# One store of the normalized tokens instead of four, and value and query weights loaded by rows of 128

## The chip, the cores and the metric

The kernel runs on one core of one Trainium2 chip. The metric is device time in microseconds (us) for one execution. Undisturbed executions of one kernel agree within one to one and a half per cent. Some are slow: they take over 1.5% more time than the fastest.

A ratio in this text is the mean time of one kernel's fast runs over the mean time of the other's fast runs of the same rounds on the same chip. It is not quite the ratio of the medians that are also quoted. The bracket behind a ratio is its 95% interval.

The engines are called by their short names in the profile. PE is TensorE, PEld its weight load, DVE VectorE, ACT ScalarE, POOL GpSimd, and SP SyncE, which computes nothing here and issues transfers. A "q" behind a name (SPq) means the engine's instruction queue.

## The reference

The input is 2,048 tokens of width 640 in bf16. One layer norm feeds two branches, and both are added to the input.

```python
def reference(x, wqkv, wo, w_gate, w_up, w_down):
    xn = layernorm(x)                        # 2048 x 640
    # A: 32 heads of 20; each token looks at itself and 7 earlier
    #    tokens, 2 apart; softmax over these 8
    q, k, v = split(xn @ wqkv)
    logits[h, s, w] = scale * sum_d q[h, s, d] * k[h, s - 2 * w, d]
    o = sum_w softmax(logits)[h, s, w] * v[h, s - 2 * w]
    # B: gated, without a nonlinearity; width 1536
    h = (xn @ w_gate) * (xn @ w_up)
    return x + o @ wo + h @ w_down
```

## The kernel before

The tokens go through in 4 chunks of 4 tiles; a tile is 128 tokens. At build time a small list scheduler in Python fixes each engine's order of instructions by estimated times. On the chip each engine then runs its list strictly in order: an instruction that waits holds up everything behind it on its engine.

The parts that matter here are these. First, the opening loads, all on SP's queue. `N2` is 320, so the value weights come as two halves of the columns of 400 KB each.

```python
    load_x(0, (0, 1))     # token tiles, 160 KB each
    load_v(0)             # value weights, first half of the columns
    load_x(0, (2,))
    load_v(N2)
    load_x(0, (3,))
    load_qkv(0)           # query weights, one transfer of 800 KB
    load_qkv(1)           # key weights
    load_x(1)
```

Second, the normalized tokens. In chunk 0 TensorE transposes them (`pst`). In chunks 1 to 3 each tile is stored to DRAM (`xnD`), and one DMA transpose reads the whole chunk back (`xnT`).

```python
def scale_x():
    xn_t = cpool.tile([P, D], BF, name="xn_t")      # 2 buffers
    nc.vector.tensor_scalar(xn_t[:], x_tiles[c * CH + ttl][:], ...)
...
def keep():                                         # once for each tile
    nc.sync.dma_start(out=xnD[tg * P : (tg + 1) * P, :], in_=st["xn", ttl][:])
    if ttl == CH - 1:
        later.append((turn_all, lambda t=clock["dve"]: t + 3.0))

def turn_all():
    nc.sync.dma_start_transpose(out=st["xnT"][:], in_=xnD[chunk c] ...)
    done["turned", c] = min(clock["pe"], clock["dve"])
```

Third, what follows the transpose of chunk 1 on the queues: the tokens of chunk 2 on SP's queue, and on POOL's software queue the output weights and down weights, 2.7 MB in all, which are called the late weights here.

```python
later.append((lambda: (load_x(2), load_down()), when(("turned", 1))))
```

`turned` is a time in the scheduler's estimate. On the chip SP waits for the store before it issues the transpose.

The attention weights. VectorE forms the products of queries and shifted keys (`pw`, six buffers), TensorE sums them by head (`lps`), ScalarE takes the exponential (`e`), VectorE masks the edge, and TensorE spreads `e` back to tokens (`eT`). On VectorE's list, the statistics and scalings of chunk 2 stand before the mask of chunk 0. A scaling that waits therefore delays the first spread.

The softmax here doesn't subtract the row's maximum and nothing guards it: scores larger than these inputs give would overflow.

Of the kernel before, what the change touches and what calls it, by code (L numbers as in the profile page):

```python
# [9 lines left out]
BF = dt.bfloat16  # L10
# [7 lines left out]
def kernel(  # L18
# [11 lines left out]
    nc = tc.nc  # L30
    P = nc.NUM_PARTITIONS
# [3 lines left out]
    S, D = x_flat.shape  # L35
# [9 lines left out]
    KT = D // P  # L45
    FT = F // P
    NT = S // P
    CH = 4
    NCH = NT // CH
    CS = CH * P  # L50
    JL = P // H
    N2 = D // 2
# [35 lines left out]
    xnD = dram.tile([S, D], BF, name="xnD")  # L88
# [4 lines left out]
    def load_x(c, ttls=range(CH)):  # L93
        for ttl in ttls:
            tg = c * CH + ttl
            x_t = cpool.tile([P, D], BF, name="x_t", bufs=6)
            nc.sync.dma_start(out=x_t[:], in_=x_flat[tg * P : (tg + 1) * P, :])
            x_tiles[tg] = x_t
# [2 lines left out]
    wg_r = B_w_gate.rearrange("(i p) f -> p i f", p=P)  # L101
    wu_r = B_w_up.rearrange("(i p) f -> p i f", p=P)

    def load_qkv(r):
        nc.sync.dma_start(
            out=wqkv[:, :, r * D : (r + 1) * D], in_=wqkv_r[:, :, r * D : (r + 1) * D]
        )

    def load_v(n0):
        cols = slice(2 * D + n0, 2 * D + n0 + N2)  # L110
        nc.sync.dma_start(out=wqkv[:, :, cols], in_=wqkv_r[:, :, cols])

    load_x(0, (0, 1))
    load_v(0)
    load_x(0, (2,))
    load_v(N2)
    load_x(0, (3,))
    load_qkv(0)
    load_qkv(1)
    load_x(1)  # L120

# [64 lines left out]
    main, chain = deque(), deque()  # L186
    burst, quick, later = [], [], []
    done = {}
    rings = {"mm": (4, []), "tr": (2, []), "lg": (1, []), "e": (1, [])}

    def when(*names):
        return lambda: max((done.get(n, INF) for n in names), default=0.0)
# [45 lines left out]
    def norm(c, group):  # L238
        st = state[c]
        st["xnT"] = None  # L240

        def alloc():
            if st["xnT"] is None:
                st["xnT"] = cpool.tile([P, KT, CS], BF, name="xnT", bufs=3)

        def steps(t0):
            g = {}

            def stats():
                g["mv"] = cpool.tile([P, group, nc.vector.BN_AGGR_DIM], F32, name="mv", bufs=2)  # L250
                for k in range(group):
                    x_t = x_tiles[c * CH + t0 + k]
                    s = cpool.tile([P, 2, nc.vector.BN_STATS_DIM], F32, name="stats")
                    for hf in range(2):
                        nc.vector.bn_stats(s[:, hf, :], x_t[:, hf * N2 : (hf + 1) * N2])  # L255
                    nc.vector.bn_aggr(g["mv"][:, k, :], s[:])
                rstd = cpool.tile([P, group], F32, name="rstd", bufs=2)
                nc.gpsimd.tensor_scalar(rstd[:], g["mv"][:, :, 1], EPS, None, op0=ALU.add)
                nc.gpsimd.tensor_tensor(
                    rstd[:], rstd[:], mhalf[:].to_broadcast([P, group]), ALU.pow  # L260
                )
                g["rstd"] = rstd

            def stats_after(t):
                on("pool", ("rstd", c, t0), t + LAG, 0.85)

            op(chain, ("stats", c, t0), stats, 1.12 * group, None, stats_after)

            def scaling(ttl, k):
                def scale_x():  # L270
                    xn_t = cpool.tile([P, D], BF, name="xn_t")
                    nc.vector.tensor_scalar(  # L272
                        xn_t[:], x_tiles[c * CH + ttl][:],
                        scalar1=g["mv"][:, k, 0:1], scalar2=g["rstd"][:, k : k + 1],
                        op0=ALU.subtract, op1=ALU.mult,
                    )
                    st["xn", ttl] = xn_t

                def turn():
                    alloc()  # L280
                    pst = ps_tr.tile([P, KT, P], BF, name="pst", tag="tr")
                    for i in range(KT):
                        nc.tensor.transpose(
                            pst[:, i, :], st["xn", ttl][:, i * P : (i + 1) * P], ident
                        )
                    nc.scalar.copy(st["xnT"][:, :, tcols(ttl)], pst[:])
                    if c == ttl == 0:
                        warm_up(14)

                def turned(t):  # L290
                    on("act", ("xnT", c, ttl), t + LAG, 0.7)

                def keep():
                    tg = c * CH + ttl
                    nc.sync.dma_start(
                        out=xnD[tg * P : (tg + 1) * P, :], in_=st["xn", ttl][:]
                    )
                    if ttl == CH - 1:
                        later.append((turn_all, lambda t=clock["dve"]: t + 3.0))

                def turn_all():
                    alloc()
                    nc.sync.dma_start_transpose(
                        out=st["xnT"][:],
                        in_=xnD[c * CS : (c + 1) * CS, :].rearrange("m (k p) -> m k p", p=P),
                    )
                    done["turned", c] = min(clock["pe"], clock["dve"])
                    for k in range(CH):
                        done["xnT", c, k] = done["turned", c] + 8.0

                def scaled(t):
                    if c >= 1:
                        later.append((keep, lambda t=t: t))
                        return
                    op(burst, ("turn", c, ttl), turn, 0.3, when(("xn", c, ttl)), turned,
                       ("tr", ("xnT", c, ttl)), 0.7)

                def later_free():
                    old = done.get(("turn", c, ttl - 2), INF)
                    if c >= 1:  # L320
                        old = done.get(("xn", c, ttl - 2), INF) + 3.0
                    return max(done.get(("rstd", c, t0), INF), old if ttl >= 2 else 0.0)

                op(chain, ("xn", c, ttl), scale_x, 0.43, later_free, scaled)

            return [lambda k=k: scaling(t0 + k, k) for k in range(group)]

        if group == 1:
            prev = None
            for t0 in range(CH):  # L330
                cur = steps(t0)
                if prev:
                    prev[0]()
                prev = cur
            prev[0]()
        else:
            for t0 in range(0, CH, group):
                for f in steps(t0):
                    f()
# [85 lines left out]
    def weights(c):  # L425
        st = state[c]
        for g in range(2):
            for j in range(JL):

                def product(g=g, j=j):  # L430
                    off = DIL * (JL * g + j)
                    pt = apool.tile([P, KT, CS], BF, name="pw", tag="pw", bufs=6)
                    nc.vector.tensor_tensor(  # L433
                        pt[:], st["qT"][:], st["kT"][:, :, off : off + CS], ALU.mult
                    )
                    st["pw", g, j] = pt

                def heads(g=g):
                    if g == 0:
                        st["e"] = apool.tile([P, 2, CS], BF, name="e", bufs=1)  # L440
                    lps = ps_log.tile([P, CS], F32, name="lps", tag="lg")
                    for i in range(KT):
                        for j in range(JL):
                            nc.tensor.matmul(  # L444
                                lps[H * j : H * (j + 1), :], lhsT=Ek[:, i, :],
                                rhs=st["pw", g, j][:, i, :],
                                start=(i == 0), stop=(i == KT - 1),
                                tile_position=(0, H * j), skip_group_check=True,
                            )
                    nc.scalar.activation(st["e"][:, g, :], lps[:], ACT.Exp, scale=scale)  # L450

                def headed(t, g=g):
                    on("act", ("exp", c, g), t + LAG, 0.6)

                def after(t, g=g, j=j, heads=heads, headed=headed):
                    if j == JL - 1:
                        op(burst, ("heads", c, g), heads, 1.2, when(("pw", c, g, j)), headed,
                           ("lg", ("exp", c, g)), 0.7)

                n = (c * 2 + g) * JL + j - 6  # L460
                free = ("heads", n // (2 * JL), n // JL % 2) if n >= 0 else None
                need = [("qk", c, 1, KT - 1)] + ([free] if free else [])
                op(chain, ("pw", c, g, j), product, 1.43, when(*need), after)

    def attend(c, ttls):
        st = state[c]
# [258 lines left out]
```

## Time and profile before

| | before |
|---|---|
| median of the first 6 runs | 272.94 us (272.09 to 274.74) |
| profiled span | 271.7 us |
| PE busy | 262.8 us, 97% |
| first query matmul on PE | 14.59 us |
| PE waits for products (`lps`) | 1.08 and 0.46 us |
| PE waits for the first spread (`eT`) | 1.76 us |
| DVE waits for stores of tokens | 14.7 us |

The first part of the profile of the kernel before gives busy time, share of the span and number of instructions for each engine.

```profile
PE 262.8 (97%) x1656; PEld 146.3 (54%) x1656; DVE 198.1 (73%) x278; ACT 101.7 (37%) x181; POOL 35.2 (13%) x77
```

PE is nearly full, so only its gaps can be won. The view of waits, for PE in the kernel before, lists them. Its columns are the waiting line, what it waited for, then the total in us, how often, and the longest.

```profile
PE eT L477 <- DVE e L469: 1.8, 1, 1.8
PE lps L444 <- DVE pw L433: 1.5, 2, 1.1
...
PE pst L283 <- DVE xn_t L272: 0.9, 1, 0.9
PE pst L283 <- POOL rstd L258: 0.4, 1, 0.4
```

The first two lines are waits for VectorE in the middle of the kernel; the last two belong to the start-up. The groups view of the kernel before tells why VectorE is late. Behind the first bar stand busy us and mean ns, behind the second the idle us before the group and what ended most of it.

```profile
L272 DVE TENSOR_SCALAR xn_t<-x_t,mv,rstd 128x640 bf16<-128x640 bf16 x16 | 6.9, 439 | 18.6 <-DMA xnD<-xn_t 14.7
```

With two buffers, the third scaling waits until the first store has landed. The timeline of DVE before, in chunk 1, shows this one by one. Columns are start, duration, instruction, and in brackets the idle time before it with its releaser.

```profile
18.76 0.80 DVE L272 TENSOR_SCALAR xn_t<-x_t,mv,rstd 128x640 bf16<-128x640 bf16 x2 [1.44 <-POOL rstd L259]
25.51 0.45 DVE L272 TENSOR_SCALAR xn_t<-x_t,mv,rstd 128x640 bf16<-128x640 bf16 x1 [5.95 <-DMA xnD<-xn_t]
28.81 0.45 DVE L272 TENSOR_SCALAR xn_t<-x_t,mv,rstd 128x640 bf16<-128x640 bf16 x1 [2.86 <-DMA xnD<-xn_t]
29.17 2.89 DVE L433 TENSOR_TENSOR pw<-qT,kT 128x2560 bf16<-128x2560 bf16 x2
```

Four scalings of 0.4 us are spread over more than 10 us, and the products of chunk 0 stand behind them. The timeline of SP's queue before shows the other end. A duration here is how long an issue holds the queue.

```profile
19.23 10.39 SPq L295 DMA_DIRECT2D xnD<-xn_t  x4
36.48 2.74 SPq L303 DMA_TRANSPOSE xnT<-xnD  x1
39.27 2.20 SPq L97 DMA_DIRECT2D x_t<-in_A_x_dram  x4
```

Stores, transpose and the load of chunk 2 follow each other in order. The transpose could not be issued before the last store had landed.

### The profile page before, as it was taken

What the parts mean: (1) busy time and instruction counts of PE and PEld (TensorE: products, weight loads), DVE (VectorE), ACT (ScalarE), POOL (GpSimd) and SP (SyncE); (2) the same over time, 40 slices, a digit from 0 to 9 for tenths busy, and PEclk for the clock granted to TensorE, in tenths of its full rate; (3) what the DMA queues carried; (4) which work ended last, traced back from release to release, by engine and by line L of the source; (5) the groups of instructions that cost most, each with busy time, mean ns of one, the idle gap of its engine ahead of it and who ended that gap; (6) DMA issues with size and microseconds to landing.
All of it is one profiled execution on the core that took longest, in us unless ns stands there. A gap on an engine that the chain in (4) does not pass through costs nothing.

```text
span 271.7 us, 4250 instructions
## 1 busy us (share of the span) xinstructions
PE 262.8 (97%) x1656; PEld 146.3 (54%) x1656; DVE 198.1 (73%) x278; ACT 101.7 (37%) x181; POOL 35.2 (13%) x77
## 2 busy tenths in 40 slices
PE   7899989979999999999999999999999999999995
PEld 7544434434645667544443577744446774445773
DVE  4460798299999965996999399799949999622221
ACT  2655545535655300255454510045551004555000
POOL 3748000200000041200000003020000212000100
PEclk9999999999999999999999999999999999999999
DMA  7999979746999925599877029959500796110111
GB/s 212 364 395 368 308 153 334 261 117 193 250 320 214 276 54 201 122 286 246 171 203 138 24 94 270 282 172 274 143 2 0 231 274 198 48 27 0 48 51 48
DMA packets 50069, 50.11 MB, mean 184 GB/s; under 512 B 20499, under 2 KB 47713, under 8 KB 50049
## 3 DMA queue, kind: packets, MB, share of 16 engines
q1 hardware_dynamic: 44704, 35.72, 49.1%
q0 software_dynamic: 3040, 11.49, 13.0%
q10 hardware_dynamic: 2304, 2.62, 2.9%
q8 instruction: 13, 0.21, 0.3%
q14 instruction: 8, 0.06, 0.1%
HBM read 35.39 MB, written 9.85 MB: 166 GB/s over the span
## 4 chain that ended last, share of the span: by engine, by line
PE 46%; DVE 26%; DMA 20%; issue 4%; SPq 2%; POOL 1%; DVEq 0%; POOLq 0%
PE psf L624 14%; PE psu L575 10%; PE psg L575 10%; DMA xnD<-xn_t 9%; PE psf L617 6%; DVE pw L433 6%; DMA x_t<-in_A_x_dram 4%; DMA v_1435<-vD 4%; DVE stats L255 3%; DMA v_912<-vD 3%; PE psv L388 2%; PE lps L444 2%; PE psqk L362 2%; DMA out_dram<-osb 1%; DVE xn_t L272 1%
## 5 line engine op out<-in xcount | busy, mean ns | idle before, releaser
L575 PE MATMUL psu<-xnT,wu 128*128 128x512 bf16 x240 | 59.7, 379 | 0.0
L575 PE MATMUL psg<-xnT,wg 128*128 128x512 bf16 x240 | 59.6, 379 | 0.0
L624 PE MATMUL psf<-wd,hT 128*128 128x320 bf16 x384 | 57.6, 299 | 0.0
L580 ACT CAST gs<-psg 128x512 bf16<-128x512 f32 x48 | 28.1, 585 | 76.1 <-PE psg L575 74.3
L433 DVE TENSOR_TENSOR pw<-qT,kT 128x2560 bf16<-128x2560 bf16 x32 | 46.1, 1485 | 0.0
L624 PEld LDWEIGHTS <-hT 128*128 128x128 bf16 x384 | 37.5, 98 | 14.9 <-issue 0.4
L362 PE MATMUL psqk<-xnT,wqkv 128*128 128x512 bf16 x200 | 44.3, 379 | 0.0
L575 PEld LDWEIGHTS <-wu 128*128 128x128 bf16 x240 | 23.2, 98 | 28.4 <-issue 1.3
L580 ACT CAST us<-psu 128x512 bf16<-128x512 f32 x48 | 28.1, 585 | 27.6 <-PE psu L575 27.6
L575 PEld LDWEIGHTS <-wg 128*128 128x128 bf16 x240 | 23.3, 98 | 27.5 <-issue 0.4
L362 PEld LDWEIGHTS <-wqkv 128*128 128x128 bf16 x200 | 19.4, 98 | 23.0 <-issue 0.4
L585 DVE TENSOR_TENSOR hT<-gs,us 128x512 bf16<-128x512 bf16 x48 | 19.7, 419 | 16.5 <-ACT us L580 16.3
L631 DVE TENSOR_TENSOR osb<-psf,xr 128x320 bf16<-128x320 f32 x32 | 15.2, 485 | 19.6 <-PE psf L624 14.2
L617 PE MATMUL psf<-wo_perm,oT 128*128 128x320 bf16 x160 | 27.0, 299 | 0.0
L641 POOL DMA_DIRECT2D out_dram<-osb x13 | 7.1, 545 | 142.3 <-DVE osb L631 139.5
L388 PE MATMUL psv<-wqkv,xnT 128*128 128x320 bf16 x160 | 23.6, 299 | 0.0
L272 DVE TENSOR_SCALAR xn_t<-x_t,mv,rstd 128x640 bf16<-128x640 bf16 x16 | 6.9, 439 | 18.6 <-DMA xnD<-xn_t 14.7
L388 PEld LDWEIGHTS <-xnT 128*128 128x128 bf16 x160 | 15.2, 98 | 6.9 <-issue 0.8
L617 PEld LDWEIGHTS <-oT 128*128 128x128 bf16 x160 | 15.5, 98 | 5.9
L255 DVE BATCH_NORM_STATS2 stats<-x_t 128x6 f32<-128x320 bf16 x32 | 13.6, 468 | 6.1 <-DMA x_t<-in_A_x_dram 6.1
L394 ACT CAST v_t<-psv 128x320 bf16<-128x320 f32 x32 | 13.6, 425 | 8.0 <-PE psv L388 6.1
L368 ACT CAST qT<-psqk 128x512 bf16<-128x512 f32 x20 | 11.7, 585 | 10.2 <-PE psqk L362 10.2
(106 smaller groups left out, 194.2 us busy)
## 6 DMA issues: line engine op xcount, KB each, us to landing
x_t<-in_A_x_dram SPq DMA_DIRECT2D x16, 160.0 KB, 3.4
vD<-v_t ACTq DMA_DIRECT2D x16, 160.0 KB, 5.3
xr<-in_A_x_dram POOLq DMA_DIRECT2D x16, 160.0 KB, 3.5
out_dram<-osb POOLq DMA_DIRECT2D x13, 160.0 KB, 3.0
wg<-in_B_w_gate_dram POOLq DMA_DIRECT2D x2, 960.0 KB, 9.8
wu<-in_B_w_up_dram POOLq DMA_DIRECT2D x2, 960.0 KB, 12.9
xnD<-xn_t SPq DMA_DIRECT2D x12, 160.0 KB, 4.4
wd<-in_B_w_down_dram POOLq DMA_DIRECT2D x1, 1920.0 KB, 11.4
```

The costliest lines, as they stand in the source:

```text
L255: nc.vector.bn_stats(s[:, hf, :], x_t[:, hf * N2 : (hf + 1) * N2])
L362: nc.tensor.matmul(ps[:], lhsT=wqkv[:, i, r * D + j * P : r * D + (j + 1) * P], rhs=st["xnT"][:, i, :], start=(i == 0), stop=(i == KT - 1),)
L368: nc.scalar.copy(dst[:, j, o : o + CS], ps[:])
L388: nc.tensor.matmul(ps[:, 0:N2], lhsT=st["xnT"][:, i, tcols(ttl)], rhs=wqkv[:, i, 2 * D + n0 : 2 * D + n0 + N2], start=(i == 0), stop=(i == ...
L394: nc.scalar.copy(v_t[:].rearrange("p (j h) -> p j h", j=Dh)[:, :, k * HH : (k + 1) * HH], ps[:, 0:N2].rearrange("p (h j) -> p j h", j=Dh),)
L433: nc.vector.tensor_tensor(pt[:], st["qT"][:], st["kT"][:, :, off : off + CS], ALU.mult)
L575: nc.tensor.matmul(ps[:], lhsT=w[:, i, f * P : (f + 1) * P], rhs=st["xnT"][:, i, :], start=(i == 0), stop=(i == KT - 1),)
L580: nc.scalar.copy(s[:], ps[:])
L585: nc.vector.tensor_tensor(h[:], st["gu", 0, f][:], st["gu", 1, f][:], ALU.mult)
L617: nc.tensor.matmul(ps[:, 0:N2], lhsT=st["oT", ttl][:, i, :], rhs=wo_perm[:, i, n0 : n0 + N2], start=(i == 0), stop=False,)
L624: nc.tensor.matmul(ps[:, 0:N2], lhsT=st["hT", f][:, tcols(ttl)], rhs=wd[:, f, n0 : n0 + N2], start=False, stop=(f == FT - 1),)
L631: nc.vector.tensor_tensor(osb[:, n0 : n0 + N2], ps[:, 0:N2], xr[:, n0 : n0 + N2], ALU.add)
```

## The change

The change has two halves that do not depend on each other. The compute is the same.

- **Store half.** In chunks 1 to 3 the four scalings write into one buffer of four tiles, which takes a place in the ring of the product buffers. One store of 640 KB replaces four of 160 KB. VectorE should no longer wait for stores.
- **Load half.** Value weights and query weights come in five transfers of 160 KB each, one for each block of 128 rows, so that TensorE can begin with the first block. Token tiles 2 and 3 now stand behind all value weights.

```diff
-    def load_qkv(r):
-        nc.sync.dma_start(
-            out=wqkv[:, :, r * D : (r + 1) * D], in_=wqkv_r[:, :, r * D : (r + 1) * D]
-        )
-    def load_v(n0): ...
+    def load_qkv(r, rows=False):
+        cols = slice(r * D, (r + 1) * D)
+        for i in range(KT) if rows else (slice(0, KT),):
+            nc.sync.dma_start(out=wqkv[:, i, cols], in_=wqkv_r[:, i, cols])
 
     load_x(0, (0, 1))
-    load_v(0)
-    load_x(0, (2,))
-    load_v(N2)
-    load_x(0, (3,))
-    load_qkv(0)
+    load_qkv(2, True)
+    load_x(0, (2, 3))
+    load_qkv(0, True)
     load_qkv(1)
     load_x(1)
 ... (in scale_x)
-                    xn_t = cpool.tile([P, D], BF, name="xn_t")
+                    if c < 1:
+                        xn_t = cpool.tile([P, D], BF, name="xn_t")
+                    else:
+                        if ttl == 0:
+                            st["xn"] = apool.tile([P, CH, D], BF, name="xn", tag="pw", bufs=6)
+                        xn_t = st["xn"][:, ttl, :]
 ... (in keep, now called once for each chunk)
-                        out=xnD[tg * P : (tg + 1) * P, :], in_=st["xn", ttl][:]
+                        out=xnD[c * CS : (c + 1) * CS, :].rearrange("(t p) d -> p t d", p=P),
+                        in_=st["xn"][:],
                     )
-                    if ttl == CH - 1:
-                        later.append((turn_all, lambda t=clock["dve"]: t + 3.0))
+                    later.append((turn_all, lambda t=clock["dve"]: t + 4.0))
 ... (the scheduler's ring for "pw" buffers, and its uses, left out)
```

Since the scheduler's estimates change, the orders on PE, DVE and ACT change a little too: on PE, head sums and spreads stand earlier.

## The prediction

> **What bounds the kernel.** TensorE. The page gives PE 262.8 of 271.7 us (97%) at full granted clock, and the windows view has it 100% busy in nearly every 20 us stretch from 60 to 240 us. So only PE's gaps are for sale. The timeline of PE lists them: start-up (first real matmul at 6.95 us, the eight value groups not done before 14.6 us, with idles of 0.44, 0.93 us), 1.08 us before the first head-sum matmuls at 35.6 us (waits for VectorE's product), 1.76 us before the first spread at 56.2 us (waits for the mask), 0.46 us at 145.3 us, and the tail after 268.7 us, which the change leaves alone. Sum of what could be won: about 4.5 us, 1.7%.
>
> **Why the gaps exist.** The first two mid-kernel gaps come from VectorE, in order behind a normalized-token write whose two buffers wait for stores. The groups view charges 14.7 us of VectorE idle to these stores; the timeline shows 5.95 and 2.86 us in chunk 1 (18.8 to 29.3 us), 4.70 in chunk 2, 1.15 in chunk 3.
>
> **What changes.** Chunks 1 to 3 write four tokens into one buffer and one 640 KB store replaces four of 160 KB; VectorE writes all four in about 1.8 us. Compute is equal. Instruction order: value/query weights take 10 queue issues instead of 3 (0.43 to 0.53 us each); spreads and head sums stand earlier on PE, by 2 to 8 us.
>
> 1. Products of chunk 0 no longer start at 29.2 us but when the keys are copied (about 26 us): three us earlier. The 1.08 us gap should vanish.
> 2. The store of chunk 1 still crawls. From 18 to 37 us the DMA view shows the software queue moving 5.20 MB in 1,288 packets (4.0 KB each), SP's queue 0.66 MB in 576 (1.1 KB each). The Trainium skill ("DMA: Bandwidth & Descriptors", Queues, rings and completion order) says that an engine alternates between queues by whole packets; the trace agrees in direction, since 160 KB took 6.3 and 7.0 us here against 1.8 us at best. One store took 6.3, two 9.2 us; extended, my estimate for 640 KB is 8 to 15 us: landing at 29 to 36 us, before 36.3. So the transpose, the load of chunk 2 and its statistics come 0 to 6 us earlier, and VectorE, ready at about 39 us, may wait for that load. The spread stands at about 48 us on PE and the mask comes at 47 to 49 us: of 1.76 us I expect 0.9 to 1.76 back.
> 3. Start-up: rows of 1,280 bytes should move faster than half rows of 640 (295 to 324 GB/s before, 367 later), but token tile 2 now queues behind all value weights (about 1 us later), and VectorE scales tile 1 only after it; tile 3 arrives about 0.6 us sooner. I count 0, plus or minus 0.6 us.
> 4. VectorE then runs 6 to 9 us ahead, but the schedule also moves PE's consumers up, so the 0.46 us gap at 145 us may stay or grow to about 1 us; value gathers (6 to 10 us each) are unchanged.
>
> Sum: 1.1 + 1.4 + 0 + 0.1 = about 2.6 us. **Predicted 270.3 us, range 268.0 to 272.8.** Faster by over 2%: 0.03; within: 0.94; slower: 0.03.
>
> **Signs.** Right: no VectorE wait on these stores; no PE wait for products near 34 us; the wait before the first spread under 1 us; PE busy time unchanged; first query matmul at 14 to 15.2 us. Wrong: a new PE wait at transposes of tile 1 near 8 us, or at head sums of chunks 1 to 3.
>
> **What would break it.** The single store landing after 37 us; value weights arriving after 8 us; head sums scheduled earlier than value gathers allow; clock throttling.

## The result, and the profile after

| | before | after |
|---|---|---|
| median of all runs beside each other | 273.55 us (40 runs, 271.51 to 275.28) | 272.64 us (20 runs, 271.09 to 293.04) |
| ratio of fast runs | | 0.9961 [0.9937, 0.9986] |
| slow runs | 0 of 40 | 3 of 20 |
| profiled span | 271.7 us | 269.4 us |
| first query matmul | 14.59 us | 15.65 us |
| last matmul group starts | 266.84 us | 264.40 us |

By the threshold of 2% the two kernels are the same. The gain is 0.4%, 1.1 us, where 2.6 us had been forecast. The profile shows 2.3 us, but the profiled execution of the changed kernel was a quick one: it took 271.46 us by the clock, against a median of 272.64, while that of the kernel before took 273.79 us against 273.55. The profile's sums are therefore used for where time went, and the timed ratios for how much.

The first part of the profile after.

```profile
PE 262.7 (98%) x1656; PEld 146.8 (54%) x1656; DVE 198.0 (73%) x278; ACT 101.8 (38%) x181; POOL 35.3 (13%) x77
```

The work is the same to 0.1 us. The waits of PE after:

```profile
PE pst L282 <- DVE xn_t L271: 1.7, 2, 1.4
...
PE eT L474 <- DVE e L466: 0.6, 1, 0.6
```

The wait for products is gone, that for the spread is down to 0.6 us, and a larger wait stands at the start-up transposes. The timeline of DVE after, to be held beside the four lines of before:

```profile
20.78 1.52 DVE L271 TENSOR_SCALAR xn<-x_t,mv,rstd 128x640 bf16<-128x640 bf16 x4 [1.44 <-POOL rstd L253]
27.26 2.90 DVE L432 TENSOR_TENSOR pw<-qT,kT 128x2560 bf16<-128x2560 bf16 x2 [4.96 <-ACT kT L367]
```

Four scalings run in 1.52 us, and VectorE then waits for the keys, not for a store. The head sums show an effect that the list of waits understates. The timeline of PE before has both of its waits inside a group of 20 head-sum matmuls:

```profile
34.11 0.40 PE L444 MATMUL lps<-pw,Ek 128*32 128x512 bf16 x3
35.59 1.24 PE L444 MATMUL lps<-pw,Ek 128*32 128x512 bf16 x17 [1.08 <-DVE pw L433]
...
144.46 0.40 PE L444 MATMUL lps<-pw,Ek 128*32 128x512 bf16 x3
145.31 1.24 PE L444 MATMUL lps<-pw,Ek 128*32 128x512 bf16 x17 [0.46 <-DVE pw L433]
```

The same group after, on the same engine:

```profile
35.17 1.26 PE L443 MATMUL lps<-pw,Ek 128*32 128x512 bf16 x20
```

In one piece the group takes 1.26 us. Broken in two it lasted from 34.11 to 36.83 and from 144.46 to 146.55 us, 2.72 and 2.09 us. So the two breaks cost 1.46 and 0.83 us, not 1.08 and 0.46. With this the profile adds up: 2.3 us at the head sums and 1.1 us at the spread (1.76 to 0.64), less 1.1 us at the start (14.59 to 15.65), make 2.3 us. The last matmul group starts 2.4 us earlier.

The start-up is where time was lost. Two timelines of the kernel before, first PE and then DVE, up to 16 us:

```profile
7.64 0.44 PE L283 MATMUL pst<-selb,xn_t 128*128 128x128 bf16 x5
9.70 0.45 PE L283 MATMUL pst<-selb,xn_t 128*128 128x128 bf16 x5 [0.93 <-DVE xn_t L272]
14.59 10.96 PE L362 MATMUL psqk<-xnT,wqkv 128*128 128x512 bf16 x50
```

```profile
6.05 0.89 DVE L255 BATCH_NORM_STATS2 stats<-x_t 128x6 f32<-128x320 bf16 x2 [0.39 <-DMA x_t<-in_A_x_dram]
13.16 0.89 DVE L255 BATCH_NORM_STATS2 stats<-x_t 128x6 f32<-128x320 bf16 x2 [2.31 <-DMA x_t<-in_A_x_dram]
```

And the same two of the kernel after:

```profile
9.39 0.45 PE L282 MATMUL pst<-selb,xn_t 128*128 128x128 bf16 x5 [1.44 <-DVE xn_t L271]
10.76 0.45 PE L282 MATMUL pst<-selb,xn_t 128*128 128x128 bf16 x5 [0.24 <-DVE xn_t L271]
15.65 10.96 PE L361 MATMUL psqk<-xnT,wqkv 128*128 128x512 bf16 x50
```

```profile
7.89 0.89 DVE L249 BATCH_NORM_STATS2 stats<-x_t 128x6 f32<-128x320 bf16 x2 [2.23 <-DMA x_t<-in_A_x_dram]
15.19 0.89 DVE L249 BATCH_NORM_STATS2 stats<-x_t 128x6 f32<-128x320 bf16 x2 [3.28 <-DMA x_t<-in_A_x_dram]
```

The statistics of token tile 2 begin at 7.89 instead of 6.05 us, since the tile now queues behind all value weights. VectorE scales tile 1 only after them, so the transpose of tile 1 on PE moves from 7.64 to 9.39 us, and the first query matmul is 1.06 us later. The first value matmul, which was meant to begin earlier with the first block of weights, came at 7.10 us against 6.95 before. The second DVE line is the arrival of chunk 1's tokens, 2.0 us later. The windows view tells of the rate. Its columns are the window, its length, busy us (with instructions) of PE, PEld, DVE, ACT and POOL, then granted clock, DMA share and GB/s. Before:

```profile
6.00:8.00 2.00, 2.00 (x29) 1.63 (x26) 1.41 (x4) 0.85 (x2) 1.01 (x3) 1.00 1.03 324
8.00:10.00 2.00, 1.07 (x13) 0.62 (x11) 1.42 (x4) 1.23 (x3) 0.74 (x3) 1.00 1.06 368
```

After:

```profile
6.00:8.00 2.00, 1.95 (x25) 1.33 (x22) 0.11 (x1) 0.70 (x2) 0.36 (x1) 1.00 0.90 271
8.00:10.00 2.00, 0.61 (x8) 0.54 (x9) 1.97 (x6) 0.54 (x2) 0.81 (x2) 1.00 0.96 282
```

The rows move at 271 to 282 GB/s, the large transfers moved at 324 to 368. From 3 to 6 us it is 260 against 295. These are single profiles: over all profiles of this case, the stretch from 8 to 10 us has 282 to 348 GB/s with rows and 361 to 379 without. Last, SP's queue after:

```profile
22.33 0.40 SPq L293 DMA_DIRECT2D xnD<-xn  x1
30.25 8.88 SPq L301 DMA_TRANSPOSE xnT<-xnD  x1
39.19 2.58 SPq L97 DMA_DIRECT2D x_t<-in_A_x_dram  x4
```

The store landed early: the transpose is issued at 30.25 us, 6.2 us sooner than before. But it now holds the queue for 8.88 us instead of 2.74, up to the moment at which the down weights land (39.1 us), and the load behind it starts at 39.19, where it had started at 39.27. All that the early store had won for the next chunk was lost again in one instruction.

### The profile page after: what moved, and what is told of

Read it like the earlier page. It is cut to its first block, busy times and chain, and to the rows that moved or that the text cites. A ratio compares the mean times of both kernels' runs of the same rounds, so it can differ in the third digit from the quotient of the medians.

```text
span 269.4 us, 4231 instructions
## 1 busy us (share of the span) xinstructions
PE 262.7 (98%) x1656; PEld 146.8 (54%) x1656; DVE 198.0 (73%) x278; ACT 101.8 (38%) x181; POOL 35.3 (13%) x77
## 4 chain that ended last, share of the span: by engine, by line
PE 80%; DMA 9%; SPq 4%; DVE 4%; POOL 1%; issue 1%; POOLq 0%
PE psf L621 19%; PE psu L572 15%; PE psg L572 15%; PE psqk L361 12%; PE psf L614 8%; PE psv L387 6%; DMA x_t<-in_A_x_dram 6%; SPq L301 3%; DMA xnD<-xn 3%; PE lps L443 3%; DVE stats L249 2%; DVE xn L271 1%; SPq L107 1%; POOL rstd L253 1%; DVE mv L250 1%
## 5 line engine op out<-in xcount | busy, mean ns | idle before, releaser
L621 PEld LDWEIGHTS <-hT 128*128 128x128 bf16 x384 | 37.5, 98 | 14.4
L387 PEld LDWEIGHTS <-xnT 128*128 128x128 bf16 x160 | 15.3, 98 | 6.6 <-issue 0.4
L367 ACT CAST kT<-psqk 128x512 bf16<-128x512 f32 x20 | 11.7, 585 | 10.2 <-PE psqk L361 10.2
```

Of the source, the lines that this page charges most:

```text
L367: nc.scalar.copy(dst[:, j, o : o + CS], ps[:])
L387: nc.tensor.matmul(ps[:, 0:N2], lhsT=st["xnT"][:, i, tcols(ttl)], rhs=wqkv[:, i, 2 * D + n0 : 2 * D + n0 + N2], start=(i == 0), stop=(i == ...
L621: nc.tensor.matmul(ps[:, 0:N2], lhsT=st["hT", f][:, tcols(ttl)], rhs=wd[:, f, n0 : n0 + N2], start=False, stop=(f == FT - 1),)
```

## The experiments

Three things were open. First, which half brings the gain and which takes it away. Second, within the load half, whether the new order or the split into rows is to blame. Third, why the transpose of chunk 1 became slow: because one big store precedes it, or because it now runs side by side with the late weights, which were nearly through by the time the old transpose was issued (POOL issued them from 23.8 to 27.2 us before and from 26.0 to 29.4 us after, and the largest took 11 us to land). Each variant kept the order of instructions on PE, DVE and ACT of the kernel that it was made from, except for the moved issues of transfers.

### Both halves apart

**The changed kernel once more**, beside the variants, on their chip.

> The changed kernel once more, on the chip of its siblings, to see how much of the profiled 2.3 us (271.7 to 269.4 us of span) is a lucky profile. My theory: the change won 1.08 (head sums), 1.1 (spread) and 0.46 us and lost 1.06 us at start-up, so a true gain of 1.0 to 2.3 us; ratio 0.992 to 0.997, span of the profile 269 to 271 us. Rival: the profiled execution was an outlier and some gaps come back in other executions: then this profile has a product or spread wait over 1 us again.

It measured 272.23 us, ratio 0.9952 [0.9918, 0.9987]; its profile spans 269.3 us, with the first query matmul at 15.75 us, the spread wait at 0.4 us and a transpose of 10.2 us. One of six runs was slow (294.71 us). The result repeats.

**The kernel before with the new loads only.**

```diff
 # kernel before, plus the load half
-    load_v(0); load_x(0, (2,)); load_v(N2); load_x(0, (3,)); load_qkv(0)
+    load_qkv(2, True); load_x(0, (2, 3)); load_qkv(0, True)
```

> The kernel before with only the new load order. Theory: the loads alone cost about 1 us: first query matmul near 15.6 us against 14.6 us, wait at the transposes of tile 1 near 1.4 us, ratio 1.002 to 1.005. Rival: loads are neutral and start-up scatters by a microsecond anyway: first query matmul 14.4 to 15 us, ratio 0.999 to 1.001.

It measured 274.67 us, ratio 1.0051 [1.0006, 1.0096]: the load half alone makes the kernel before slower by 1.4 us. The waits of PE:

```profile
PE eT L471 <- DVE e L463: 2.6, 1, 2.6
PE pst L277 <- DVE xn_t L266: 1.8, 2, 1.6
PE lps L438 <- DVE pw L427: 1.4, 1, 1.4
```

The waits for the spread and at the start-up transposes are longer than before; that for products is 1.4 us once, where it was 1.08 and 0.46 us. Its profile fell on the slowest of its six runs (277.04 us), so the 2.6 may be at the upper end; a repeated profile of the kernel before had 2.6 there as well.

**The changed kernel with the old loads**, that is the store half alone.

```diff
 # changed kernel, loads as before
-    load_qkv(2, True); load_x(0, (2, 3)); load_qkv(0, True)
+    load_v(0); load_x(0, (2,)); load_v(N2); load_x(0, (3,)); load_qkv(0)
```

> The changed kernel with the old load order (column halves of the value weights, token tiles 2 and 3 in between). Theory: gains add up: first query matmul back at 14.6 us, no product wait, spread wait under 1.2 us; ratio to before 0.988 to 0.993, about 1 us better than the changed kernel. Rival: an earlier start only moves the waits: the spread waits 1 us longer, and the time stays that of the changed kernel, 0.995 to 0.997.

It measured 270.62 us, ratio 0.9909 [0.9872, 0.9946]. That is 2.5 us of 273.25 (the median of before in these rounds), nearly the whole forecast of 2.6. Its waits of PE:

```profile
PE pst L288 <- DVE xn_t L277: 1.3, 2, 0.8
...
PE eT L480 <- DVE e L472: 0.2, 1, 0.2
```

No wait for products, 0.2 us at the spread, and the first query matmul at 14.43 us. So the store half, with the order that goes with it, does what was hoped, and the load half takes back 1.2 us (0.9952 against 0.9909) to 1.4 us.

### Order or split

**The new order, but value and query weights in one transfer each.**

```diff
-    load_qkv(2, True)
+    load_qkv(2)
     load_x(0, (2, 3))
-    load_qkv(0, True)
+    load_qkv(0)
```

> The changed kernel with value and query weights by one transfer each instead of five, in the same order (tiles 2 and 3 behind the whole value weights). It parts the split from the order. If the split costs (many issues, lower rate; windows showed 260 to 282 GB/s at 3 to 10 us against 295 to 368 before): tile 2 lands at 6.8 to 7.2 us instead of 7.9, first query matmul near 14.6 to 15 us, chunk 1 tokens land before 14 us instead of 15.2. If the order costs: tile 2 still at 7.6 us or later and the first query matmul at 15.3 us or later.

It measured 271.29 us, ratio 0.9935 [0.9899, 0.9972]. The timeline of DVE has the two arrivals:

```profile
7.81 0.89 DVE L249 BATCH_NORM_STATS2 stats<-x_t 128x6 f32<-128x320 bf16 x2 [2.13 <-DMA x_t<-in_A_x_dram]
...
13.49 0.89 DVE L249 BATCH_NORM_STATS2 stats<-x_t 128x6 f32<-128x320 bf16 x2 [1.66 <-DMA x_t<-in_A_x_dram]
```

Token tile 2 is as late as with rows (7.81), and the first query matmul too (15.57). But chunk 1's tokens arrive at 13.49, 1.7 us sooner than with rows, the stream runs at 314 to 368 GB/s between 6 and 10 us, and the spread does not wait. So there are two costs: the order delays the start, and the split into rows slows the stream, which chunk 1 feels. Whether the split costs through smaller transfers or through the issues (SP needs about 0.46 us for each of ten, instead of for two) was not tested.

**Rows, but with the token tiles between them**, the fourth corner.

```diff
         for i in range(KT) if rows else (slice(0, KT),):
+            if r == 2 and i in (2, 4):
+                load_x(0, (1 + i // 2,))
             nc.sync.dma_start(out=wqkv[:, i, cols], in_=wqkv_r[:, i, cols])
-    load_x(0, (2, 3))
```

> The changed kernel, value and query weights still by rows of 128, but token tile 2 after the second of the five value rows and tile 3 after the fourth, about as they stood before the change. It completes the square of split and order. Theory (two costs: the order delays tile 2 and so the value groups; the split slows the stream and so chunk 1's tokens): statistics of tile 2 start near 6.1 to 6.8 us instead of 7.9, first query matmul at 14.6 to 15.2 us instead of 15.4 to 15.9, while chunk 1's tokens still land at 14.8 us or later; ratio to before 0.991 to 0.994. Rival (the split alone costs, order does not): tile 2 still at 7.4 us or later and the first query matmul at 15.4 us or later; ratio 0.995 or more.

It went wrong in a way that nothing here had foretold: five of six runs were slow, the median was 280.68 us (271.08 to 286.26), and no ratio could be formed. The early part can still be read: tile 2 at 6.27 us and the first query matmul at 14.62, as with the old order, and chunk 1's tokens at 15.33, as with rows. The fast profile of these loads with later weights, below, agrees: 5.72, 14.41 and 15.43 us. The two costs are separable. The slowness had to be looked at by itself, below.

By time the order costs about 0.7 us (0.9909 to 0.9935) and the split about 0.5 us (0.9935 to 0.9952). The intervals of these ratios overlap, so neither of the two is clear of noise by itself. Two versions with rows and with the late weights issued later, both described below, part the order once more, on different chips: 0.9923 with the tiles between, 0.9985 with them behind. What makes the partition more than a guess is the times in the traces. In the six profiles whose tile 2 queues behind all value weights its statistics begin at 7.6 to 8.1 us and the first query matmul comes at 15.4 to 15.9 us; in the ten others these are 5.7 to 6.8 and 14.4 to 15.3. In the eight profiles with rows chunk 1's tokens arrive at 15.2 to 16.2 us, in the eight others at 13.0 to 13.9.

**Both tiles between the two halves of the value weights**, on the store half alone.

```diff
 # store half alone
     load_v(0)
-    load_x(0, (2,))
+    load_x(0, (2, 3))
     load_v(N2)
-    load_x(0, (3,))
```

> Old loads with the collected store, but tokens 2 and 3 both before the second half of the value weights. Theory (start-up is set by when tile 3 has landed, since VectorE takes its statistics before it scales tile 2): tile 3 lands near 7.3 us instead of 8.0, first query matmul about 0.3 to 0.4 us earlier (14.0 to 14.2 us), ratio 0.001 lower than that of the collected store with old loads. Rival: the second half of the value weights becomes the limit near 8 us: a wait at the second value group, first query matmul at 14.4 us or later.

It measured 270.17 us, 0.9895 [0.9863, 0.9927]; the first query matmul stayed at 14.53 us and the spread waited 1.1 us in this profile. This is not to be told from the store half alone.

### Why the transpose was slow

**The late weights issued later**, after the statistics of chunk 2 in VectorE's list.

```diff
-    later.append((lambda: (load_x(2), load_down()), when(("turned", 1))))
+    later.append((lambda: load_x(2), when(("turned", 1))))
 ...
     norm(2, 4)
+    side(load_down)
```

> The changed kernel with the output and down weights (2.7 MB, on the software queue) issued after the statistics of chunk 2 instead of beside the store and transpose of chunk 1. Theory: that traffic made the transpose of chunk 1 hold SP's queue for 8.9 to 10.2 us; without it the issue takes 2.6 to 3.0 us as in the other chunks, the load of chunk 2 starts at 31 to 34 us instead of 39 to 40.5, VectorE no longer waits for it (3.1 to 3.4 us before), the mask is written by about 48 us and the spread wait (0.4 to 0.6 us) is gone; time 0.4 to 0.6 us better than the changed kernel, ratio to before about 0.993. Rival: the transpose is slow because it follows a single big store; then it still takes 8 us or more.

SP's queue in this variant:

```profile
30.81 2.65 SPq L301 DMA_TRANSPOSE xnT<-xnD  x1
33.52 1.99 SPq L97 DMA_DIRECT2D x_t<-in_A_x_dram  x4
...
54.31 6.96 SPq L301 DMA_TRANSPOSE xnT<-xnD  x1
```

Without late weights beside it the transpose of chunk 1 takes 2.65 us, and the load of chunk 2 is out at 33.52 instead of 39.19. The store before it is the same single one of 640 KB, so the store is not the cause. POOL issued the late weights at 46.2 to 49.7 us instead, and the slow transpose moved to chunk 2 (6.96 us). The traces show one thing more. In all ten fast profiles in which a transpose is issued over 3 us before the down weights land, it holds the queue until the down weights land, within 1.3 us (39.13 and 39.1 us in the changed kernel, 61.27 and 60.6 us here). How long it holds the queue thus followed how much of the weights was left. The new wait is on PE, at the head sums of chunk 1:

```profile
86.79 1.24 PE L443 MATMUL lps<-pw,Ek 128*32 128x512 bf16 x17 [1.03 <-DVE pw L432]
```

VectorE was late there because it had waited 3.2 us for a gather of values (the shifted values of a tile, read back from DRAM) until 68.9 us; it was issued on SP's queue after the slow transpose. The spread did not wait any more, but the time was 272.63 us, ratio 0.9985 [0.9945, 1.0026]: nothing won. The weights have to pass somewhere, and at both places tried they met a transpose and SP's queue stood.

**The same on the store half alone.**

> Old load order, collected store, and late output and down weights: all three findings together. Theory: start-up as before the change (first query matmul 14.4 to 14.6 us), no product wait, no spread wait; but the collected store with old loads had only 0.2 us of spread wait left, so the time is at most 0.3 us better than that kernel: ratio to before 0.988 to 0.991. Rival: weights that move beside the value gathers of chunk 0 (42 to 56 us) delay these, and a new wait appears on VectorE before the first mixes or on TensorE at the head sums of chunk 1: ratio 0.992 or more.

It measured 272.37 us, 0.9967 [0.9934, 0.9999], worse than 0.9909 without the edit. The transposes of chunks 1 and 2 took 2.69 and 7.27 us, and PE waited 1.4 us for products near 85 us. The pattern is the same.

**The tokens of chunk 2 issued ahead of the transpose**, on the changed kernel.

```diff
 # in keep, after the store
+                    if c == 1:
+                        load_x(2)
 ...
-    later.append((lambda: (load_x(2), load_down()), when(("turned", 1))))
+    later.append((load_down, when(("turned", 1))))
```

> The changed kernel with the load of chunk 2's tokens issued before the transpose of chunk 1 rather than behind it; all other traffic as it was. Theory: VectorE's wait of 3.1 to 3.4 us for those tokens vanishes, whatever the transpose does (its issue stays 8 us or more, or grows, since the tokens move beside it); the spread wait vanishes; ratio about 0.993. Rival: what holds the spread is something else (the value weights' late start), then the spread wait stays at 0.4 us or more although the tokens are early.

It measured 271.16 us, 0.9926 [0.9879, 0.9972]. The transpose was even slower, as its line on SP's queue shows, but the load no longer stood behind it:

```profile
30.43 13.52 SPq L303 DMA_TRANSPOSE xnT<-xnD  x1
```

Statistics of chunk 2 began at 40.1 instead of 43.8 us and the spread did not wait. So what the spread still waited in the changed kernel (0.4 to 0.6 us) could be had by taking the load from behind the transpose.

**The same on the store half alone.**

> The collected store with the old loads, and chunk 2's tokens loaded ahead of the transpose of chunk 1. Theory: no product and no spread wait in any case; the transpose holds SP's queue for 9 us or more, so the value gathers of chunk 0 start 2 to 3 us later than with the collected store alone, with little loss (a VectorE wait of at most 2 us at a mix): ratio to before 0.987 to 0.991, that is 0 to 0.6 us better than the collected store with old loads. Rival: late gathers cost as much as the early tokens give: ratio 0.991 or more, with a product wait of 0.6 us or more at the head sums of chunk 1.

It measured 269.91 us (269.5 to 271.17), 0.9894 [0.9864, 0.9924], the lowest median of all. The spread did not wait; a wait of 0.9 us for products appeared later.

**The late weights from ACT's queue instead of POOL's**, on the store half alone. This was to show whether it matters how the late weights are issued and cut into packets.

```diff
-            nc.gpsimd.dma_start(out=wo_perm[...], in_=wo_r[jl])
-        nc.gpsimd.dma_start(out=wd[:], in_=...)
+            nc.scalar.dma_start(out=wo_perm[...], in_=wo_r[jl])
+        nc.scalar.dma_start(out=wd[:], in_=...)
```

> The collected store with the old loads; the output and down weights issued by ScalarE's hardware queue instead of the software queue, same bytes, nearly the same moment (4 issues of about 0.35 us and one more on ScalarE). If the transpose is slow because the software queue's 4 KB packets take most of each round, then beside 1.1 KB packets its issue takes 3 to 6 us instead of 9 to 10 us and chunk 2's tokens land 3 us or more earlier. Rival: it is slow because any 2.7 MB beside it fill the engines: the issue still takes 8 us or more. ScalarE's casts of the keys should be held up by about 1 to 2 us once, without a wait on TensorE. Ratio to before 0.988 to 0.993 under either.

It measured 282.64 us, 1.0357 [1.0321, 1.0393], and does not answer the question. ACT's queue held the four issues of the output weights for 12.93 us, and the copy of the keys stood behind them:

```profile
22.91 12.93 ACTq L173 DMA_DIRECT2D wo_perm<-in_A_wo_dram  x4
```

PE waited 10.0 us for the keys. The transpose took 2.89 us here, but at 30.22 us the down weights were not yet under way (ACT issued them at 35.87 us), so the meeting that was to be tested did not take place. Why exactly a transpose slows down beside these weights is left open.

**The kernel before once more**, for the scatter of a single profile.

> The kernel before, profiled a second time, since the profiles of the change (2.3 us) and the timed ratio (1.1 to 1.3 us) differ. If the waits of the first profile are typical: a spread wait of 1.4 to 2.1 us, a product wait of 0.8 to 1.4 us and a first query matmul at 14.4 to 15.3 us. If the first profile was an unlucky execution: spread and product waits sum to under 2 us and the span is 271 us or less.

273.75 us in one run, with a span of 271.7 us again. The first query matmul came at 14.97 instead of 14.59 us, the spread waited 2.6 instead of 1.8 us and the head sums 0.6 instead of 1.1. So single waits move by up to 0.9 us between two profiles of one kernel, while their sum (3.3 and 3.2 us for products and spread) and the span stayed.

### Slow executions

In the first trace of rows with tiles between, TensorE waited 8.9 us for the first spread. Two more kernels were run: the same again, and the same with the late weights issued later as above.

> The same kernel as the slow one, once more, on the chip of its sibling. If the collapse belongs to this kernel, three or more of six executions are over 276 us again and a profile of one has the spread wait over 5 us; fast ones lie at 270 to 272 us. If it was the chip of that day, all are at 270 to 273 us, ratio to before 0.990 to 0.995, with the first query matmul at 14.5 to 15.2 us.

> Rows of weights with token tiles 2 and 3 in between, and the output and down weights issued after the statistics of chunk 2. The run without the last edit was slow in 5 of 6 executions (279 to 286 us); its profile shows the transfers at 37 to 103 GB/s from 37 to 45 us, the transpose of chunk 1 landing after 17.7 us and TensorE idle for 8.9 us at the spread, at full clock until then. Theory: that collapse needs the transpose and the weights of the software queue side by side; parted, no execution is over 275 us, the transpose is issued within 3 us, first query matmul at 14.5 to 15.3 us; ratio to before near that of the changed kernel with late weights or up to 0.004 lower (0.994 to 0.998), since the head sums of chunk 1 wait about 1 us as there. Rival: the order of loads itself, or the chip, makes it slow: most executions are again over 278 us.

The repetition was slow in five of six runs, median 287.68 us (272.06 to 292.82). Its profile fell on a slow run too. Four lines of its windows, columns as above, and the line of PE at the spread from the timeline:

```profile
35.00:40.00 5.00, 5.00 (x34) 2.11 (x23) 4.49 (x5) 2.36 (x5) 0.00 (x0) 1.00 1.06 63
...
45.00:50.00 5.00, 4.84 (x23) 1.99 (x21) 0.00 (x0) 0.65 (x2) 0.00 (x0) 1.00 1.12 118
50.00:55.00 5.00, 0.00 (x0) 0.00 (x0) 0.00 (x0) 0.00 (x0) 0.00 (x0) 0.82 1.28 96
55.00:60.00 5.00, 0.00 (x0) 0.00 (x0) 0.48 (x2) 0.00 (x0) 0.00 (x0) 0.50 1.01 134
```

```profile
67.19 0.32 PE L475 MATMUL eT<-selb,e 128*128 128x160 bf16 x1 [17.35 <-DVE e L467]
```

SP's queue in the same trace:

```profile
30.69 11.72 SPq L302 DMA_TRANSPOSE xnT<-xnD  x1
```

From 35 to 40 us the DMA engines count as fully busy and move 63 GB/s; the down weights took 28 us to land. The load of chunk 2's tokens, behind it, held the queue for 7.11 us more, and PE idled for 17.35 us. Only after PE had stopped did its clock fall to 0.50. The lower clock of this run is a consequence of the idle time, not its cause; the idle time alone is about as long as what this run took more than the one fast run of its kernel (288.74 against 272.06 us). The Trainium skill ("TensorE: Matmul & The Clock Gate", Part 1, What's actually happening) says that the clock goes to half after at least one idle window of about 3.4 us. This trace agrees: PE's last matmul ended at 49.84 us, and the 0.82 of the window from 50 to 55 us, worked out as full clock followed by half, puts the fall at 53.2 us, 3.4 us later.

With the late weights parted from the transpose of chunk 1 none of six runs was slow: 271.3 us (271.13 to 271.82), ratio 0.9923 [0.9888, 0.9957]. The transpose in its trace:

```profile
29.78 3.04 SPq L302 DMA_TRANSPOSE xnT<-xnD  x1
```

Together that is 10 slow runs of 12 with the late weights beside that transpose and 0 of 6 with them later, on the same chip as the repetition. So for this variant the collapse belongs to the late weights running beside the transpose of chunk 1. It is not any meeting of the two: later, the same weights met the transpose of chunk 2 (4.46 us on the queue) without a collapse, and the two fast profiles of the changed kernel show the meeting without a collapse. One difference: POOL issued the down weights at 31.15 and 30.43 us in the two slow traces, close to the transpose's 30.75 and 30.69, and at 28.29 in the changed kernel, 2 us before it. Whether that matters was not tested.

The changed kernel has slow runs of its own, 3 of 20 and 1 of 6 (276.01, 287.76, 293.04 and 294.71 us), where the kernel before had none of 40. That they have the same cause is likely, but none of them was profiled, so it is not shown. In the ten other versions, the kernel before left out, none of 56 runs was slow. The slow runs are not small: the mean of all 20 runs is 274.50 us, above the 273.60 of the kernel before. The ratio of fast runs hides this by its definition.

## Why the prediction was right or wrong, point by point

The median, 272.64 us, lies in the range, close to its upper end, and the call "within 2%" held. But the gain is 0.4% where 1.0% was forecast.

1. **Step 1 (products start earlier, 1.1 us): right, and a little too small.** DVE's scalings took 1.52 us in a row, the wait for products vanished. The products started 1.9 us earlier (27.26 instead of 29.17) and not three, since the keys came later with the start-up. The gap was worth 1.46 us, since a broken group of head sums costs more than its wait.
2. **Step 2 (0.9 to 1.76 us back at the spread): the size was right, the path half wrong.** The spread wait fell by 1.1 us. The store landed after 7.9 us, at the lower edge of the estimate of 8 to 15. But nothing of that reached chunk 2: "the transpose, the load of chunk 2 and its statistics come 0 to 6 us earlier" became 0.1 us for the load and 1.0 us later for the statistics (42.78 to 43.75). The prediction had tacitly taken the transpose at its old duration. The gain came from the other side: the scalings of chunk 2 no longer waited 4.7 us for stores ahead of the mask. That the size came out right was in part luck. The transpose's duration with and without the late weights beside it (8.9 against 2.65 us) is shown by the runs.
3. **Step 3 (start-up, 0 plus or minus 0.6 us): this is the step that failed.** It measured a loss of 1.06 us in the profile, outside the bounds, and 1.2 to 1.4 us in time. Both of its halves were in the text: tile 2 "about 1 us later" (it was 1.8 us), and VectorE's scaling of tile 1 behind it, which the trace shows. They were set off against "rows of 1,280 bytes should move faster than half rows of 640", and that is wrong here: 260 to 282 GB/s with rows, 295 to 368 before. Nor did the length of a row show by itself: whole transfers moved 288 GB/s from 3 to 6 us with rows of 1,280 bytes, and 266 and 295 in the two profiles of the kernel before. I looked at the length of a row in memory and not at the size of a transfer. Two 400 KB transfers and one of 800 KB had become ten of 160 KB. The Trainium skill ("DMA: Bandwidth & Descriptors", Rules for kernel authors) advises to coalesce many small transfers into one large one; the case agrees, with 271 and 282 GB/s split and 314 and 368 whole in the same windows and the same order, though the cost of the issues is not parted from it.
4. **Step 4 (the 0.46 us gap may stay or grow, 0.1 us): too cautious.** It vanished, and with the mended group it was worth 0.83 us in the profile.

Sum: of 2.6 us the store half alone brought 2.5, so the terms of the store half were sized well together. The term of the start-up, counted as 0, was minus 1.2 to 1.4. The signs were well chosen: the wait at the transposes of tile 1 near 8 us, named as a sign of being wrong, is the one that appeared (1.44 us before 9.39), and the first query matmul at 15.65 us missed the 14 to 15.2 that would have been right.

The prediction also used the skill's statement ("DMA: Bandwidth & Descriptors", Queues, rings and completion order) that engines alternate between queues by whole packets. The runs agree that a transfer on SP's queue slows beside the software queue (the transpose held it for 8.88 us against 2.65). That packet size is the reason was not shown; the run meant for it was inconclusive.

Versions that beat both kernels: the store half alone (270.62 us, 0.9909), with both tiles between the halves of the value weights (270.17, 0.9895), or with chunk 2's tokens ahead of the transpose (269.91, 0.9894). The three can't be told from each other, none of their 18 runs was slow, and by the threshold of 2% all are the same as the kernel before.

## What to carry to other kernels

Judge each half of a change by its own critical resource: here the store half was worth about twice the whole change, and a load half that looked neutral took half of it back. Where a transfer is brought forward, ask what it will then run beside: a transpose that had followed a large weight load now ran beside it and held its queue three times as long (8.88 against 2.74 us), until the load had landed. Look at slow runs too before saying that a kernel is better, since a ratio of fast runs can't show a new risk of stalling.

## What the Trainium skill lacked or had wrong

- "DMA: Bandwidth & Descriptors" has no figure for how long a DMA transpose of this size holds the queue that issues it, or for what other traffic does to that. Here a transpose of 640 KB held SP's queue for 2.6 to 3.5 us where the weights of the software queue were through or nearly so, and for 4.5 to 14.2 us beside 2.7 MB of them, in the fast profiles until these had landed.
- The same page, Rules for kernel authors, says that a transpose next to ordinary DMAs "needs nothing". The row is about correct data, and that held: all results here were correct. It says nothing of time: besides the longer hold, ten of twelve runs of one variant were slow (one profile fell to 63 GB/s with the engines counted as busy), and none of six once the late weights were moved away.
- The same page, Issuing engines are not separate DMA queues, calls the time to initiate a DMA "usually small relative to the DMA itself". Here four issues of output weights of 200 KB each held ACT's queue for 12.93 us in all, where POOL had issued the same four in 2.33 us. The kernel with them on ACT took 3.6% more than the kernel before; without that edit it took 0.9% less.
